# Attention and two feed-forward layers on one core: weights routed through PSUM, query sums copied by a DMA, one more key tile on GpSimd

## The chip, the cores and the metric

The kernel runs on one core of a Trainium2 chip. The metric is device time in microseconds (us) of one execution; lower is better. TensorE does the matmuls, VectorE (DVE), ScalarE (ACT) and GpSimd (POOL) the elementwise work, and SyncE (SP) issues all transfers. The granted TensorE clock was 0.999 of full speed over the profiled execution, which is its upper level, 2.4 GHz.

## The reference

```
q_pool = q.reshape(2, 8, 576, 2, 64).mean(axis=3)      # pairs of queries are averaged; seq is 1152
scores = q_pool @ k.transpose(0, 1, 3, 2) / sqrt(64)
attn = exp(scores - max); attn = attn / (sum(attn) + 1e-09)
x = (attn @ v), heads side by side                     # 1152 tokens x 512
h = x @ w_in (512 x 2048);   g = h if h >= 1, 0 if h <= -1, else (h+1)**2 / 4;   x = g @ w_out
h = x @ w_in2 (512 x 2048);  g = h * sigmoid(h);                                 out = g @ w_out2
```

Inputs are float32, except that the four weight matrices arrive in 64-bit form, two 32-bit words (`low`, `top`) a value.

## The kernel before

Every product is done with operands split into two parts (`hi` and `lo = x - hi`), and three or fewer of the four cross products, so each operand costs a copy and a subtraction. All work is first recorded as a list of `op(target, ways, deps, bufs, both)`: a way is an engine, how long the engine is held, the latency, and the function that emits the instructions. `plan_out` then lists them: again and again it takes the engine whose next piece could start first, by its own table of durations, free buffers (`room`) and due times, and writes the instructions in that order into each engine's queue. So a changed duration or rule reorders every engine; on the chip each queue runs in that order and waits where data are late.

- Attention runs over 16 heads. Of each head, `inputs` loads q, k and v and splits them: `split_q` adds the two queries of a pair (written twice side by side, `qs`, so that one transpose gives two stacked copies), PE transposes, and `qm` holds the query parts. `scores` multiplies 128 queries by 3 x 384 keys into a PSUM bank, DVE takes it out with a running minimum (L562), ACT does the exponential (L575).
- `values` takes the 9 key tiles of a head one by one: 4 PE transposes into a bank (L610), then `split` into the parts `thl`, then the matmuls with `vhl` (L618). `KINDS` says for each key tile how `split` goes. "psum": ACT writes `hi` from the bank (L588), DVE subtracts from the bank (L589). "pool": ACT copies the bank to `pf` (L593), GpSimd makes `hi` (L594) and `lo` (L135). Queries left over from two heads form `tails`, scaled in `ztail` (L670). `invert` adds 1e-9 to the sums on GpSimd (L687) and inverts them on DVE.
- Six PSUM banks (`b`) are shared by all of this; two more (`y`) hold the running output.
- The weights of a group of the hidden layer (there are 8, `w` = 0 to 7) come in quarters of 128 x 512. `weight_tasks` rebuilds float32 from the two words: ACT takes the absolute value (`size`, L102), DVE does `clamp` (L105), `shift` (L109), `sign` (L113) and `rest` (L117) on the tile `wf` in SBUF, ACT makes `hi` (L125), GpSimd `lo` (L135). The eight quarters of group 0 are worked off during attention, four of w_in between the heads and four of w_out at its end; those of groups 1 to 7 during the feed-forward part.
- The feed-forward part is 96 steps, `gemm1` (L155) and `gemm2` (L200 and L202), with five elementwise operations between them. Its first four `gemm1` stand among the last head's work.

`both` marks a DVE operation that works on SBUF alone. The planner held such an operation back while it thought GpSimd busy:

```
if o.both and e == "DVE" and pool_until[0] <= s < pool_until[1]:
    s = pool_until[1]
```

Of the kernel before, what the change touches and what calls it, by code (L numbers as in the profile page):

```python
# [18 lines left out]
def fused_kernel(  # L19
# [36 lines left out]
    KINDS = ("psum", "pool", "psum", "pool", "psum", "pool", "psum", "pool", "psum")  # L56
# [20 lines left out]
    def weight_tasks(idx, kind, pools, RAWS):  # L77
# [6 lines left out]
        def quarter(c):  # L84
            st = {}

            def load():
                if c == 0:
                    wt[layer, g, kind] = [
                        parts.tile([P, 4, 512], F32R, tag=f"w{x}{kind}", name=f"w{x}{kind}") for x in "hl"  # L90
                    ]
                if kind == "i":
                    sv = src[c * P : (c + 1) * P, g * FG * 2 : (g + 1) * FG * 2]
                else:
                    sv = src[g * FG + c * P : g * FG + (c + 1) * P, :]
                raw = raws.tile([P, 512, 2], U32, tag="wr", name="wr", bufs=RAWS)
                nc.sync.dma_start(out=raw.rearrange("p f w -> p (f w)"), in_=sv)
                st["low"], st["top"] = raw[:, :, 0], raw[:, :, 1]

            def size():  # L100
                st["w"] = raws.tile([P, 512], F32, tag="wf", name="wf", bufs=RAWS)
                nc.scalar.activation(st["w"], st["top"].bitcast(F32), AF.Abs)  # L102

            def clamp():
                nc.vector.tensor_scalar(st["w"], st["w"], LEAST, MOST, ALU.max, ALU.min)  # L105

            def shift():
                wi = st["w"].bitcast(U32)
                nc.vector.tensor_scalar(wi, wi, 3, 0x3FFFFFF8, ALU.logical_shift_left, ALU.bitwise_and)  # L109

            def sign():
                wi = st["w"].bitcast(U32)
                nc.vector.scalar_tensor_tensor(wi, st["top"], 0xC0000000, wi, ALU.bitwise_and, ALU.bitwise_or)  # L113

            def rest():
                wi = st["w"].bitcast(U32)
# [12 lines left out]

            return load, size, clamp, shift, sign, rest, parts_of, part_hi, part_lo  # L130
# [131 lines left out]
    def plan_out():  # L262
# [21 lines left out]
        while len(made) < len(ops):  # L284
            best = None
            for e in engines:
                found = []
                for o, k, t in ready[e].values():
# [12 lines left out]
                    if o.both and e == "DVE" and pool_until[0] <= s < pool_until[1]:  # L301
                        s = pool_until[1]
# [14 lines left out]
            if e == "POOL":  # L317
                pool_until = (s, s + lat)
            made.append(o)
# [19 lines left out]
    with ExitStack() as at, ExitStack() as keys, ExitStack() as prep:  # L339
# [27 lines left out]
        ztail = fixed.tile([P, P], F32, name="ztail")  # L367
        room.update(qraw=2, kraw=2, vraw=1, khl=2, qs=2, kk=3, qm=2, qt=2, qtraw=2, qts=1, p=2 * NM, pt=1, thl=THL, pf=PF, vhl=2)
# [6 lines left out]
        def prepare():  # L375
            nc.vector.tensor_copy(ident_r, ident)
            nc.vector.tensor_add(jtail, ident[:, 0:D], ident[:, D : 2 * D])
# [22 lines left out]
        def inputs(h):  # L400
# [33 lines left out]
            for part in [slice(3 * g, 3 * g + 3) for g in range(3)] if h == 0 else [slice(0, KC)] * 1:  # L434
# [5 lines left out]
                if first:  # L440
                    ways.insert(0, ("DVE", 0.1 + 0.6 * n, 0.18 + 0.6 * n, lo(nc.vector)))
                klo.append(op(t1 + 0.01, ways, [khi[-1]], [kr, kb], both=first))
# [25 lines left out]
            def split_q(e):  # L468
                t = qraws[qr.slot]
                e.tensor_add(qss[qb.slot], *(t[:, :, r].unsqueeze(2).to_broadcast([P, NM, 2, D]) for r in range(2)))  # L470

            t3 = base(h - 2) - 0.1 * PERIOD
            ways = [("POOL", 1.25, 1.31, lambda: split_q(nc.gpsimd))]
            if first:
                ways.insert(0, ("DVE", 0.6, 0.69, lambda: split_q(nc.vector)))
            sq = op(t3, ways, [lq], [qr, qb], both=first)
# [157 lines left out]
        def tails(h):  # L634
# [35 lines left out]
            o2 = op(t1 + 0.4, ("DVE", 0.2, 0.28, lambda: nc.vector.tensor_scalar_mul(ztail, ztail, sums[key])), [o1, o_inv[key]], [zb], both=True)  # L670
# [9 lines left out]
        def invert(h):  # L680
# [88 lines left out]

        STAGES = (("ACT", 0.57, 0.672), ("DVE", 0.332, 0.42), ("DVE", 0.335, 0.427), ("DVE", 0.6, 0.69), ("DVE", 0.6, 0.69))  # L770
        w_last = [None]

        def weights(w, kind, times, deps):


            def get(n, m):
                if (w, kind) not in wsets:
# [4 lines left out]
                    wsets[w, kind] = weight_tasks(w, kind, pools, 1 if (w, kind) == (0, "i") else RAWS)  # L782
# [4 lines left out]
            made = []  # L787
            for n, t in enumerate(times):
                bufs = [Buf("w" if (w, kind) == (0, "i") else "raw"), *whole]
                prev = op(t - 5, ("SP", 2.0, 4.4, lambda n=n: get(n, 0)()), [*deps, w_last[0]], bufs)  # L790
                w_last[0] = prev
                for m, (e, occ, lat) in enumerate(STAGES):
                    prev = op(t + 0.3 * m, (e, occ, lat, lambda n=n, m=m: get(n, m + 1)()), [prev], bufs, both=e == "DVE")
# [114 lines left out]
```

## Time and profile before

| | us |
|---|---|
| median of 3 runs | 695.96 (695.18 to 696.7) |
| profiled execution | 693.9 |
| its span, first to last instruction | 692.1 |
| TensorE busy in the span | 678.8 (98%) |
| VectorE, GpSimd, ScalarE busy | 547.1, 431.2, 413.7 |

A row of the trace names a source line, the engine, the operation and the tiles it writes and reads (`out<-in`). An engine's "idle before" is time in which it had nothing running; the name behind the arrow is what ended it. Matmuls are pipelined, so a busy TensorE is not one at its peak.

### The profile page before, as it was taken

To read this page: it belongs to the slowest core of one execution; us is meant where nothing else is said; L and a number is where in the kernel's file an instruction comes from. 1 tells how busy PE (TensorE), PEld (TensorE's weight loads), DVE (VectorE), ACT (ScalarE), POOL (GpSimd) and SP (SyncE) were. 2 spreads that over 40 slices of the span, in tenths; PEclk is the share of its full clock that TensorE was granted. 3 is DMA by queue.
4 is the path that set the end of the run, shared out by engine and by line. 5 is a ranking of instruction groups with operands and counts; after the bars stand their busy time and mean duration, and the time that the engine had idled before them with its cause. 6 is when DMAs were issued, how large, how long until landed. Compare 5 with 4: busy or idle time off the path is not lost.

```text
span 692.1 us, 11265 instructions
## 1 busy us (share of the span) xinstructions
PE 678.8 (98%) x3959; PEld 627.4 (91%) x3959; DVE 547.1 (79%) x1205; ACT 413.7 (60%) x773; POOL 431.2 (62%) x406
## 2 busy tenths in 40 slices
PE   8999999999999998999999999999999999999997
PEld 6898989888989997899999999999898999999896
DVE  7889989898888889658999796897884894993223
ACT  7988997968797887545544444454554543442221
POOL 7959897969796757735654455478664554453221
PEclk9999999999999999999999999999999999999999
DMA  7332231222110032102332232122131221200012
GB/s 210 109 92 59 92 112 38 79 72 65 50 49 11 26 124 76 62 31 92 122 123 91 92 106 79 61 92 92 62 121 62 92 93 60 93 30 1 1 45 92
DMA packets 28489, 52.93 MB, mean 76 GB/s; under 512 B 4752, under 2 KB 13968, under 8 KB 28432
## 3 DMA queue, kind: packets, MB, share of 16 engines
q1 hardware_dynamic: 28432, 52.21, 23.6%
q8 instruction: 31, 0.51, 0.3%
q14 instruction: 26, 0.21, 0.1%
HBM read 49.81 MB, written 2.39 MB: 75 GB/s over the span
## 4 chain that ended last, share of the span: by engine, by line
PE 81%; DVE 8%; POOL 7%; issue 2%; ACT 1%; DMA 0%; SPq 0%; POOLq 0%; DVEq 0%; ACTq 0%
PE bank L155 27%; PE bank L200 14%; PE bank L202 14%; PE bank L555 9%; PE bank L618 7%; PE bank L610 6%; DVE p L562 2%; POOL thl L135 2%; PE bank L656 2%; POOL xl L135 1%; POOL thl L594 1%; DVE thl L589 1%; PE bank L454 1%; PE bank L647 1%; DVE wf L113 1%
## 5 line engine op out<-in xcount | busy, mean ns | idle before, releaser
L135 POOL TENSOR_TENSOR gl<-gf,gh 128x384 fp32r<-128x384 f32 x96 | 112.4, 1171 | 119.2 <-ACT gh L184 117.5
L155 PE MATMUL bank<-xh,whi 128*128 128x384 f32 x384 | 129.2, 337 | 0.0
L155 PE MATMUL bank<-xl,whi 128*128 128x384 f32 x384 | 129.2, 336 | 0.0
L155 PE MATMUL bank<-xh,wli 128*128 128x384 f32 x384 | 128.9, 336 | 0.0
L562 DVE TENSOR_SCALAR_CACHE_REDUCE p<-bank 128x384 f32<-128x384 f32 x192 | 101.3, 550 | 18.8 <-PE bank L555 17.5
L618 PE MATMUL bank<-thl,vhl 128*128 128x512 f32 x288 | 112.4, 433 | 2.8 <-DVE thl L589 1.5
L178 DVE TENSOR_TENSOR gf<-bank,gf 128x384 f32<-128x384 f32 x96 | 52.9, 551 | 61.6 <-ACT gf L170 57.7
L555 PE MATMUL bank<-kk,qm 128*128 128x384 f32 x384 | 95.3, 352 | 1.9 <-DVE thl L589 1.7
L610 PE MATMUL bank<-ident,p 128*128 128x128 f32 x576 | 85.3, 273 | 0.0
L135 POOL TENSOR_TENSOR thl<-pf,thl 128x512 fp32r<-128x512 f32 x64 | 83.1, 1298 | 3.3
L575 ACT ACTIVATE p<-p,low 128x1152 f32<-128x1152 f32 x64 | 81.0, 1266 | 5.7 <-DVE low L572 5.5
L184 ACT CAST gh<-gf 128x384 fp32r<-128x384 f32 x96 | 49.4, 514 | 53.1 <-DVE gf L178 52.0
L113 DVE SCALAR_TENSOR_TENSOR wf<-wr,wf 128x512 uint32<-128x512 uint32 x64 | 76.2, 1191 | 1.2
L610 PEld LDWEIGHTS bank<-ident,p 128*128 128x128 f32 x576 | 69.4, 140 | 7.8 <-DVE thl L589 0.3
L555 PEld LDWEIGHTS bank<-kk,qm 128*128 128x128 f32 x384 | 65.4, 189 | 10.7 <-DVE thl L589 3.3
L155 PEld LDWEIGHTS bank<-xl,whi 128*128 128x128 f32 x384 | 72.1, 188 | 2.1
L155 PEld LDWEIGHTS bank<-xh,whi 128*128 128x128 f32 x384 | 72.1, 188 | 2.0
L155 PEld LDWEIGHTS bank<-xh,wli 128*128 128x128 f32 x384 | 72.1, 188 | 0.0
L589 DVE TENSOR_TENSOR thl<-bank,thl 128x512 fp32r<-128x512 f32 (+1 forms) x104 | 66.8, 653 | 3.6 <-ACT thl L588 3.3
L588 ACT CAST thl<-bank 128x512 fp32r<-128x512 f32 (+1 forms) x104 | 57.1, 562 | 20.6 <-PE bank L610 16.7
L170 ACT ACTIVATE gf<-bank 128x384 f32<-128x384 f32 x48 | 23.6, 492 | 76.5 <-PE bank L155 73.2
L135 POOL TENSOR_TENSOR wli<-wf,whi 128x512 fp32r<-128x512 f32 x32 | 43.1, 1347 | 41.7 <-ACT whi L125 41.5
(90 smaller groups left out, 1537.7 us busy)
## 6 DMA issues: line engine op xcount, KB each, us to landing
wr<-in_moe_w_in_dram SPq DMA_DIRECT2D x32, 512.0 KB, 3.7
wr<-in_moe_w_out_dram SPq DMA_DIRECT2D x32, 512.0 KB, 3.3
kraw<-in_k_dram SPq DMA_DIRECT2D x16, 288.0 KB, 2.9
vraw<-in_v_dram SPq DMA_DIRECT2D x16, 288.0 KB, 2.8
qraw<-in_q_dram SPq DMA_DIRECT2D x16, 256.0 KB, 3.0
out_dram<-part SPq DMA_DIRECT2D x9, 256.0 KB, 2.0
rb<-row SPq DMA_DIRECT2D x16, 128.0 KB, 3.3
qtraw<-in_q_dram SPq DMA_DIRECT2D x16, 32.0 KB, 2.5
```

What stands on the lines that cost most here:

```text
L113: nc.vector.scalar_tensor_tensor(wi, st["top"], 0xC0000000, wi, ALU.bitwise_and, ALU.bitwise_or)
L135: eng.tensor_sub(out, whole, hi.bitcast(F32))
L155: nc.tensor.matmul(ps, lhsT=w[:, c, j * P : (j + 1) * P], rhs=a[:, c, ts_], start=(c == 0 and n == 0), stop=(c == ND - 1 and n == 2),)
L200: nc.tensor.matmul(ps[:, :TB], lhsT=w[:, j, m * P : (m + 1) * P], rhs=a, start=start, stop=stop)
L202: nc.tensor.matmul(ps, lhsT=a[:, m * P : (m + 1) * P], rhs=w[:, j, :], start=start, stop=stop)
L555: nc.tensor.matmul(ps, lhsT=qq[:, c0 : c0 + P], rhs=rhs, start=n == 0, stop=n == last)
L562: nc.vector.tensor_scalar(dst, ps, -1.0, None, ALU.mult, ALU.min, accum_out=mxs[key, t][:, j : j + 1])
L575: nc.scalar.activation(pt(), pt(), AF.Exp, bias=lows[key][:, tt : tt + 1], scale=-1.0, accum_out=sums[key][:, tt : tt + 1])
L588: o1 = op(target, ("ACT", 0.477 * f, 0.587 * f, lambda: nc.scalar.copy(th(), ps())), deps, [bank, tb])
L589: o2 = op(target + 0.3, ("DVE", 0.6 * f, 0.683 * f, lambda: nc.vector.tensor_sub(tl(), ps(), th().bitcast(F32))), [o1], [bank, tb])
L610: nc.tensor.transpose(banks[bank.slot][:, i * P : (i + 1) * P], ps_[p_of[h, i].slot][:, c * P : (c + 1) * P], ident)
L618: nc.tensor.matmul(banks[6 + yb.slot], lhsT=lhsT, rhs=thls[tb.slot][i], start=not count, stop=len(count) == 2 * KC - 1)
```

## The change

- `clamp` and `shift` of group 0's quarters write a PSUM bank (`via`), `sign` works on it, `rest` reads it and writes `wf` again. The bank is one of the six (`b`), held from `clamp` to `rest`. All other groups stay in SBUF.
- The planner lets a `both` operation of DVE hold GpSimd as well, and keeps it off GpSimd 0.1 us earlier. `FAR`, the costs of the PSUM route, are not `both`.
- `split_q` writes the sum once; a DMA on SP's queue copies it beside itself (not for head 0).
- The last of the nine key tiles of a head goes the "pool" way.
- The scaling of `ztail` and the addition of 1e-9 go to ACT; the low part of head 1's keys is GpSimd's alone.

```diff
-    KINDS = ("psum", "pool", "psum", "pool", "psum", "pool", "psum", "pool", "psum")
+    KINDS = ("psum", "pool", "psum", "pool", "psum", "pool", "psum", "pool", "pool")
...
             def clamp():
-                nc.vector.tensor_scalar(st["w"], st["w"], LEAST, MOST, ALU.max, ALU.min)
+                st["x"] = via[c]() if c in via else st["w"]
+                nc.vector.tensor_scalar(st["x"], st["w"], LEAST, MOST, ALU.max, ALU.min)
             def shift():
-                nc.vector.tensor_scalar(wi, wi, 3, 0x3FFFFFF8, ALU.logical_shift_left, ALU.bitwise_and)
+                nc.vector.tensor_scalar(xi, xi, 3, 0x3FFFFFF8, ALU.logical_shift_left, ALU.bitwise_and)
             def sign():
-                nc.vector.scalar_tensor_tensor(wi, st["top"], 0xC0000000, wi, ALU.bitwise_and, ALU.bitwise_or)
+                nc.vector.scalar_tensor_tensor(xi, st["top"], 0xC0000000, xi, ALU.bitwise_and, ALU.bitwise_or)
             def rest():
-                nc.vector.scalar_tensor_tensor(wi, st["low"], 29, wi, ALU.logical_shift_right, ALU.bitwise_or)
+                nc.vector.scalar_tensor_tensor(wi, st["low"], 29, xi, ALU.logical_shift_right, ALU.bitwise_or)
...
-                    if o.both and e == "DVE" and pool_until[0] <= s < pool_until[1]:
+                    if o.both and e == "DVE" and pool_until[0] - 0.1 <= s < pool_until[1]:
...
             if e == "POOL":
                 pool_until = (s, s + lat)
+            elif o.both and e == "DVE":
+                free["POOL"] = max(free["POOL"], s + lat - 0.1)
...
+                if h:
+                    e.tensor_add(qss[qb.slot][:, :, 0], t[:, :, 0], t[:, :, 1])
...
+                twice = lambda: nc.sync.dma_start(out=qss[qb.slot][:, :, 1], in_=qss[qb.slot][:, :, 0])
...
-            o2 = op(t1 + 0.4, ("DVE", 0.2, 0.28, lambda: nc.vector.tensor_scalar_mul(ztail, ztail, sums[key])), [o1, o_inv[key]], [zb], both=True)
+            o2 = op(t1 + 0.4, ("ACT", 0.17, 0.28, lambda: nc.scalar.mul(ztail, ztail, sums[key])), [o1, o_inv[key]], [zb])
...
-                o = op(t0, ("POOL", 0.284, 0.23, lambda: nc.gpsimd.tensor_scalar_add(sums[key], sums[key], 1e-9)), deps)
+                o = op(t0, ("ACT", 0.1, 0.21, lambda: nc.scalar.activation(sums[key], sums[key], AF.Identity, bias=tiny)), deps)
...
+        FAR = (("ACT", 0.57, 0.672), *[("DVE", 0.6, 0.69)] * 4)
...
+                bank = Buf("b")
+                if not w:
+                    via[n] = lambda bank=bank: banks[bank.slot]
...
+                for m, (e, occ, lat) in enumerate(STAGES if w else FAR):
+                    more = bufs if w or not m else [*bufs, bank]
+                    prev = op(t + 0.3 * m, (e, occ, lat, lambda n=n, m=m: get(n, m + 1)()), [prev], more, both=e == "DVE" and w > 0)
```

The plan moves instructions everywhere in the attention part; from the second third of the first feed-forward layer on TensorE's order is the same. Three places matter below. The first is VectorE's queue at the fourth w_in quarter of group 0. Before, `rest` (L117) stood straight ahead of a key tile's subtraction (L589):

```order
L629 TENSOR_TENSOR y_143<-bank_77,pf_139 64x512
L572 TENSOR_REDUCE low<-mx 128x1
L117 SCALAR_TENSOR_TENSOR wf<-wr,wf 128x512
L589 TENSOR_TENSOR thl_133<-bank_73,thl_132 128x512
L677 TENSOR_TENSOR xl<-bank_71,xh 128x64
```

In the changed kernel the same quarter (`sign` is L115, `rest` L119, the subtraction L600) stands so in VectorE's queue, its intermediate in a bank:

```order
L600 TENSOR_TENSOR thl_137<-bank_75,thl_136 128x512
L115 SCALAR_TENSOR_TENSOR bank_74<-wr,bank_74 128x512
L573 TENSOR_SCALAR p_126,mx<-bank_70 128x384
L119 SCALAR_TENSOR_TENSOR wf<-wr,bank_74 128x512
L640 TENSOR_TENSOR y_142<-bank_77,pf_139 64x512
L600 TENSOR_TENSOR thl_131<-bank_73,thl_130 128x512
```

The operation still has a subtraction behind it; what moved is the tile that it reads and writes. `clamp` of this quarter stands 12 rows ahead of L115, and bank_74 is held from there to L119.

The second place is TensorE's queue at the last key tile of the last head, whose second part is thl_133. Before, its matmul (L618) came ahead of the first `gemm2` (L200):

```order
L618 MATMUL bank_77<-thl_132,vhl_141 128x512
L618 MATMUL bank_77<-thl_131,vhl_141 128x512
L618 MATMUL bank_77<-thl_133,vhl_141 128x512
L200 MATMUL bank_70<-gh,who 128x384
L200 MATMUL bank_70<-gl,who 128x384
```

In the changed kernel (L629 for L618, L202 for L200) nine matmuls of `gemm2` stand between the two parts of that tile:

```order
L629 MATMUL bank_77<-thl_132,vhl_141 128x512
L202 MATMUL bank_71<-gh,who 128x384
L202 MATMUL bank_71<-gl,who 128x384
L202 MATMUL bank_71<-gh,wlo 128x384
L202 MATMUL bank_72<-gh,who 128x384
L202 MATMUL bank_72<-gl,who 128x384
L202 MATMUL bank_72<-gh,wlo 128x384
L202 MATMUL bank_73<-gh,who 128x384
L202 MATMUL bank_73<-gl,who 128x384
L202 MATMUL bank_73<-gh,wlo 128x384
L629 MATMUL bank_77<-thl_133,vhl_141 128x512
```

The wait for thl_133 moved behind work that doesn't need it.

The third place is SP's queue around one head's copy of the query sums. Before:

```order
L97 DMA wr<-in_moe_w_in_dram 128x1024
L700 DMA row<-sum 128x4
L703 DMA rb_145<-row 64x512
L414 DMA qraw_98<-in_q_dram 128x4x128
L429 DMA vraw_105<-in_v_dram 128x576
```

And in the changed kernel (L711 and L714 are the sums' two transfers, L420 and L435 the loads of q and v):

```order
L711 DMA row<-sum 128x4
L97 DMA wr<-in_moe_w_in_dram 128x1024
L714 DMA rb_144<-row 64x512
L484 DMA qs_108<-qs_108 128x4x64
L420 DMA qraw_98<-in_q_dram 128x4x128
L435 DMA vraw_105<-in_v_dram 128x576
```

The copy (L484) waits on SP for GpSimd's addition, and the next loads of q and v stand behind it.

## Rows read from the trace of the kernel before

**Rows 1.** Windows, attention part: length, busy us of PE, PEld, DVE, ACT, POOL.

```profile
0.00:292.00 292.00, 283.78 (x1853) 253.03 (x1854) 253.99 (x780) 240.61 (x441) 233.26 (x245) 1.00 0.27 79
...
120.00:160.00 40.00, 36.95 (x241) 32.02 (x240) 35.54 (x105) 33.02 (x63) 33.62 (x33) 1.00 0.24 69
260.00:292.00 32.00, 28.86 (x175) 25.56 (x174) 27.16 (x57) 20.45 (x40) 24.86 (x24) 1.00 0.23 71
```

**Rows 2.** Timeline of TensorE, eight stretches: start, length, in brackets idle and releaser.

```profile
148.92 0.45 PE L454 MATMUL bank<-ident_r,khl 128*128 128x128 f32 x3 [0.70 <-DVE p L562]
...
159.22 0.62 PE L555 MATMUL bank<-kk,qm 128*128 128x384 f32 x2 [1.72 <-DVE thl L589]
...
261.28 0.44 PE L555 MATMUL bank<-kk,qt 128*128 128x384 f32 x1 [0.58 <-DVE low L572]
...
266.97 0.43 PE L675 MATMUL bank<-jtail,ztail 128*128 128x64 f32 x2 [0.60 <-DVE ztail L670]
...
273.41 0.50 PE L618 MATMUL bank<-thl,vhl 128*128 128x512 f32 x1 [0.76 <-DVE thl L589]
...
284.69 0.50 PE L618 MATMUL bank<-thl,vhl 128*128 128x512 f32 x1 [0.53 <-POOL thl L135]
...
290.04 0.49 PE L618 MATMUL bank<-thl,vhl 128*128 128x512 f32 x1 [0.64 <-DVE thl L589]
...
357.48 0.44 PE L200 MATMUL bank<-gh,who 128*128 128x384 f32 x1 [0.83 <-DVE part L214]
```

**Rows 3.** Timeline ahead of 159.22: VectorE, then GpSimd.

```profile
156.49 2.07 DVE L117 SCALAR_TENSOR_TENSOR wf<-wr,wf 128x512 uint32<-128x512 uint32 x1
...
156.47 1.54 POOL L720 TENSOR_TENSOR y<-y,rb 128x512 f32<-128x512 f32 x1 [0.18 <-DVE y L629]
157.97 1.74 POOL L470 TENSOR_TENSOR qs<-qraw 128x512 f32<-128x512 f32 x1
```

**Rows 4.** Groups of VectorE by line and form, 0 to 292 us.

```profile
L589 DVE TENSOR_TENSOR thl<-bank,thl 128x512 fp32r<-128x512 f32 x96 | 65.2, 684 | 3.6 <-ACT thl L588 3.3
...
L117 DVE SCALAR_TENSOR_TENSOR wf<-wr,wf 128x512 uint32<-128x512 uint32 x8 | 10.5, 1308 | 0.0
L113 DVE SCALAR_TENSOR_TENSOR wf<-wr,wf 128x512 uint32<-128x512 uint32 x8 | 9.2, 1151 | 0.0
L109 DVE TENSOR_SCALAR wf<-wf 128x512 uint32<-128x512 uint32 x8 | 5.9, 733 | 0.0
...
L105 DVE TENSOR_SCALAR wf<-wf 128x512 f32<-128x512 f32 x8 | 4.2, 532 | 0.0
```

**Rows 5.** Line 105 alone, same stretch: shortest, median and longest duration in ns.

```profile
L105 DVE TENSOR_SCALAR wf<-wf x8: 394/414/1174, 58.5 to 269.3; 128x512 f32<-128x512 f32 x8
```

**Rows 6.** Groups of GpSimd by line and form, 0 to 292 us.

```profile
L135 POOL TENSOR_TENSOR thl<-pf,thl 128x512 fp32r<-128x512 f32 x64 | 83.1, 1298 | 3.3
L594 POOL CAST thl<-pf 128x512 fp32r<-128x512 f32 x64 | 42.5, 663 | 24.3 <-ACT pf L593 21.6 <-PE bank L610 2.3
...
L470 POOL TENSOR_TENSOR qs<-qraw 128x512 f32<-128x512 f32 x15 | 19.7, 1320 | 4.4 <-PE bank L481 3.6 <-DMA qraw<-in_q_dram 0.7
...
L687 POOL TENSOR_SCALAR sum<-sum 128x4 f32<-128x4 f32 x16 | 3.9, 245 | 6.5 <-ACT p L575 5.7
...
L687 POOL TENSOR_SCALAR sum<-sum 128x1 f32<-128x1 f32 x8 | 2.3, 287 | 0.9 <-DVE wf L109 0.3
```

**Rows 7.** Waits of TensorE, 0 to 292 us: total, times, longest.

```profile
PE bank L618 <- POOL thl L135: 0.8, 2, 0.5
PE bank L454 <- DVE p L562: 0.7, 1, 0.7
...
PE bank L618 <- POOL thl L594: 0.4, 2, 0.2
```

**Rows 8.** Chain that ended last, in order of time: start, length, what.

```profile
293.05 4.22 PE bank L200 x24
```

**Rows 9.** DMA issues: KB each, median us to landing.

```profile
rb<-row SPq DMA_DIRECT2D x16, 128.0 KB, 3.3
```

More of the change, by code (lines that the diff above doesn't have):

```diff
@@ L75, in fused_kernel, with weight_tasks @@
     wt = {}
-    def weight_tasks(idx, kind, pools, RAWS):
+    def weight_tasks(idx, kind, pools, RAWS, via):
         layer, g = seq[idx]
@@ L367, in fused_kernel @@
         ztail = fixed.tile([P, P], F32, name="ztail")
+        tiny = fixed.tile([P, 1], F32, name="tiny")
         room.update(qraw=2, kraw=2, vraw=1, khl=2, qs=2, kk=3, qm=2, qt=2, qtraw=2, qts=1, p=2 * NM, pt=1, thl=THL, pf=PF, vhl=2)
@@ L376, in prepare @@
             nc.vector.tensor_copy(ident_r, ident)
+            nc.vector.memset(tiny, 1e-9)
             nc.vector.tensor_add(jtail, ident[:, 0:D], ident[:, D : 2 * D])
@@ L439, in inputs @@
                 ways = [("POOL", 0.2 + 1.175 * n, 0.25 + 1.18 * n, lo(nc.gpsimd))]
-                if first:
+                if not h:
                     ways.insert(0, ("DVE", 0.1 + 0.6 * n, 0.18 + 0.6 * n, lo(nc.vector)))
-                klo.append(op(t1 + 0.01, ways, [khi[-1]], [kr, kb], both=first))
+                klo.append(op(t1 + 0.01, ways, [khi[-1]], [kr, kb], both=not h))
             if h:
@@ L469, in split_q @@
                 t = qraws[qr.slot]
-                e.tensor_add(qss[qb.slot], *(t[:, :, r].unsqueeze(2).to_broadcast([P, NM, 2, D]) for r in range(2)))
+                if h:
+                    e.tensor_add(qss[qb.slot][:, :, 0], t[:, :, 0], t[:, :, 1])
+                else:
+                    e.tensor_add(qss[qb.slot], *(t[:, :, r].unsqueeze(2).to_broadcast([P, NM, 2, D]) for r in range(2)))
             t3 = base(h - 2) - 0.1 * PERIOD
[L473 to L476, printed above, removed]
+            if h:
+                sq = op(t3, ("POOL", 0.7, 0.76, lambda: split_q(nc.gpsimd)), [lq], [qr, qb])
+                twice = lambda: nc.sync.dma_start(out=qss[qb.slot][:, :, 1], in_=qss[qb.slot][:, :, 0])
+                sq = op(t3 + 1, ("SP", 0.5, 2.6, twice), [sq], [qb])
+            else:
+                sq = op(t3, [("DVE", 0.6, 0.69, lambda: split_q(nc.vector)), ("POOL", 1.25, 1.31, lambda: split_q(nc.gpsimd))], [lq], [qr, qb], both=True)
             t4 = base(h - 2) + 0.3 * PERIOD
@@ L786, in weights @@
             whole = [Buf("w" + kind)] if w else []
-            made = []
+            made, via = [], {}
             for n, t in enumerate(times):
                 bufs = [Buf("w" if (w, kind) == (0, "i") else "raw"), *whole]
+                bank = Buf("b")
+                if not w:
+                    via[n] = lambda bank=bank: banks[bank.slot]
                 prev = op(t - 5, ("SP", 2.0, 4.4, lambda n=n: get(n, 0)()), [*deps, w_last[0]], bufs)
                 w_last[0] = prev
-                for m, (e, occ, lat) in enumerate(STAGES):
-                    prev = op(t + 0.3 * m, (e, occ, lat, lambda n=n, m=m: get(n, m + 1)()), [prev], bufs, both=e == "DVE")
+                for m, (e, occ, lat) in enumerate(STAGES if w else FAR):
+                    more = bufs if w or not m else [*bufs, bank]
+                    prev = op(t + 0.3 * m, (e, occ, lat, lambda n=n, m=m: get(n, m + 1)()), [prev], more, both=e == "DVE" and w > 0)
                 prev = op(t + 2, ("ACT", 0.51, 0.61, lambda n=n: get(n, 7)()), [prev], bufs)
```

8 lines of the change are left out of this document (4 added, 4 removed).

## The prediction

> **What bounds the kernel now.** I read the windows first. TensorE is busy for 678.8 of the 692.1 us of the span. After 292 us, where the feed-forward part begins, it is short of work only at 357.48 (0.83 us) and once more by less. The attention part before that has 292 - 283.78 = 8.22 us of idle TensorE, and it lies in few places: 40 - 36.95 = 3.05 us in the window from 120 to 160, and 32 - 28.86 = 3.14 us in the window from 260 to 292 [rows 1]. The stretch between these two and the one from 20 to 120 are at TensorE's pace. So no change here can bring much more than some 8 us, unless it takes work from TensorE, which this one doesn't.
>
> Then I read TensorE's timeline for the places in question. Seven idle stretches in the two windows, of 0.53 to 1.72 us, are ended by VectorE six times and by GpSimd once [rows 2]. The timelines of these two engines say what came ahead. Before the longest one, at 159.22, VectorE spends 2.07 us on one `rest` (L117), from 156.49 on. GpSimd runs L720 and then L470 in that time, the latter in 1.74 us [rows 3]. The subtraction L589 for which TensorE waits stands straight behind `rest`, and TensorE starts when it is done. L117 has a mean of 1308 ns there, L113 one of 1151, while L589, of the same 128x512 and with one operand in PSUM, has 684 [rows 4]. L105 takes between 394 and 1174 ns for the same work [rows 5]; L470 has a mean of 1320 against its 1.74 [rows 6]. I read this as VectorE and GpSimd holding each other up when both work on SBUF alone, and a form that reads PSUM as free of it. The planner's table has 0.69 us for L117, so it let the transposed scores behind it come late.
>
> **The change, part by part.** All sums are made against the profiled execution, 693.9 us, whose span is 692.1; the median of the runs shown is 695.96, 2.06 more, and I add that at the end.
>
> *Weights through a bank.* A quarter's four operations now take 532 + 733 + 1151 + 1308 = 3724 ns [rows 4, 5]. Through PSUM I price each like L589: 4 x 684 = 2736 ns. That is 0.99 us a quarter, 7.9 us of VectorE for eight, none of it on TensorE's path by itself. What counts is the long operation ahead of a wait. Six of the stretches, 0.70 + 1.72 + 0.58 + 0.60 + 0.76 + 0.53 = 4.89 us [rows 2], stand where quarters are worked off; the seventh, at 290.04, comes below. The nearest row for the new forms is L589, which also writes SBUF; nothing in this trace writes a bank from VectorE with weights in it. Bounds: nothing comes back (0), or all idle of both windows, 3.05 + 3.14 = 6.19. I take -4.9.
>
> One rule speaks against this part. L105 undisturbed takes 394 to 414 ns [rows 5], and L589 684 [rows 4]. The Trainium skill, VectorE: DVE Perf Modes, section Why PSUM operands drop a tier, says that an fp32 operation with any operand in PSUM loses the mode that uses both SBUF ports, and does one element a cycle. By it, `clamp` and `shift` through a bank can't keep their short form: 16 x (0.684 - 0.414) = 4.3 us more of VectorE than if nothing disturbed them. The measured means, with the disturbance, leave a gain in the sum of four. If the disturbance had been absent where it mattered, this part would be worth 0.
>
> *One more key tile for GpSimd.* Sixteen tiles move from ACT and VectorE's L589 to ACT and GpSimd's L594 and L135. Each costs GpSimd 663 + 1298 = 1961 ns [rows 6], 31.4 us together, and frees 16 x 0.684 = 10.9 us of VectorE. A tile's parts are ready 1.961 - 0.684 = 1.28 us later. GpSimd is given back about half of L470, by elements written 0.66 us of 1.32, 15 x 0.66 = 9.9, and L687's 16 x 0.245 = 3.9 [rows 6] (eight smaller ones left out). So it goes from 233.26 to 233.3 + 31.4 - 9.9 - 3.9 = 250.9 us of 292, 86% [rows 1]. VectorE goes from 253.99 to 254.0 - 10.9 - 7.9 = 235.2, 81%. GpSimd becomes the fullest of the three helpers. The 64 tiles that go this way now cost TensorE 0.8 + 0.4 = 1.2 us of waits in all [rows 7], 0.02 each, since the planner puts other matmuls between. Sixteen more at that price are 0.3; with GpSimd's idle share nearly a third smaller (20% to 14%) I take +1.0. Bounds: 0, and all of the latency uncovered, 16 x 1.28 = 20.5.
>
> *The last tile of the last head.* It is where a longer latency would show, as there is little attention work behind it. At 290.04 TensorE waits 0.64 us for L589 [rows 2]. In the new order nine matmuls of `gemm2` stand between the two parts. Such a matmul takes 4.22 / 24 = 0.176 us [rows 8], so they cover 1.58 us, more than the 1.28. I take 0: one wait for another. Without that cover it would be +1.28.
>
> *The copy of the query sums.* A head's `qs` is complete later by the copy: half an addition (0.66) and a transfer of 128 KB that I price like the one of rb, of the same size, 3.3 us to landing [rows 9], against 1.32 before: 0.66 + 3.3 - 1.32 = +2.6 us. `qs` is not in the list of what TensorE waits for [rows 7], because the planner makes it a head ahead; 0. Behind it on SP's queue stand the next loads of q and v, and nothing late depends on them within a head. Uncovered it would be 15 x 2.6 = 39 us, a bound that I leave out of the range, since a whole head of other matmuls lies between.
>
> *The planner's rule.* In the feed-forward part weights stay in SBUF. There the rule can only move VectorE's operations away from GpSimd's. At 357.48 TensorE loses 0.83 us to VectorE [rows 2]; I give it half, -0.4. The move of `ztail` and the 1e-9 to ACT costs ACT under 10 us of the 292 - 240.61 that it has free [rows 1]: 0.
>
> Sum: -4.9 + 1.0 + 0 + 0 - 0.4 = -4.3. The profiled execution comes to 689.6, the median to 691.7.
>
> **The rivals.** *The disturbance stays* (or was not the cause). GpSimd is busier, and if `rest` still runs long because it writes SBUF and reads `wr` there, the stretches remain: -0.4 + 1.0, about 696. Against it: L589 also reads one SBUF operand and writes SBUF, and its mean of 684 stands among the same GpSimd work [rows 4]. The Trainium skill, SBUF — State Buffer, section Who interferes with whom, says that only a port pair shared by VectorE and GpSimd contends, as an exclusive lock; by that an operation that needs one SBUF read and one write of its own is free of it. The trace agrees for L589; no row shows it for an operation that writes a bank. Chance 0.10, between 694.6 and 697.
>
> *GpSimd becomes the bound* (the other side). At 86% mean it will be at its limit in stretches where heads overlap with weights, and TensorE then waits for L135 at many of the sixteen tiles. With x us exposed at each the result is -5.3 + 16x: slower by more than can be measured from x = 0.42 on (16 x 0.42 = 6.7). At 0.5 it is +2.7, 698.7. For it: two waits on L135 already [rows 7]. Against it: these are 0.8 in all, and the planner chooses matmuls by GpSimd's durations. 0.09.
>
> *A bank is missing.* For each quarter one of the six banks is held while 8 to 14 rows of VectorE's queue go by, at about 0.68 each some 8 us [rows 4], 64 us for eight. If TensorE were held by banks all that time it would lose a sixth, 10.7 us; half of that gives -4.3 + 5.4 = +1.1, 697.0. For it: a wait of 0.7 us on `p` L562, which empties a bank [rows 7]. Against it: it is the only long one that ends on taking scores out. 0.07, half of it slower.
>
> **How the numbers follow.** The forecast, faster, has a chance of 0.74 and a range of its own of 687.5 to 694.4: from all of 6.19 and 0.83 and a bit of start-up returned to less than half of the 4.9, where it would no longer be told from no change. A measurement of this kernel can tell about 0.2%, 1.4 us. Faster by more than that 0.74, within it 0.14 (the first rival and half of the third, 0.10 + 0.035), slower 0.12 (the second and the other half). The range reaches to 696.5, which takes in the first rival and leaves out the second; below it stops at 687.5, as there is no more idle time to give back.
>
> **What the profile after would show.** Right: windows with nearly no idle of TensorE around the two stretches of weights; the four operations at 0.6 to 0.75 us each with a longest near the mean; L135 on `thl` about 80 times and waits of TensorE on it below 2 us in all; GpSimd near 250 us and VectorE near 235 in the attention part. Wrong: `rest` with single values over 1 us; waits on `thl` of GpSimd at 0.3 us or more, many times; waits of TensorE on banks held by weights; a late transpose of `qs`; or a start-up that got longer, for which I have no row.

## The result, and the profile after

The changed kernel took 685.62 us (median of 4 runs, 685.51 to 685.7), the kernel before 695.73 in the same comparison (695.18 to 696.7): a ratio of 0.9853, interval 0.9836 to 0.987. That is 10.1 us faster, below the range of 687.5 to 696.5. The profiled execution went from 693.9 to 685.5, its span from 692.1 to 683.7.

The windows of the changed kernel (columns as in [rows 1]):

```profile
0.00:292.00 292.00, 288.42 (x1899) 260.76 (x1900) 236.89 (x757) 249.62 (x480) 242.91 (x254) 1.00 0.31 85
120.00:160.00 40.00, 39.85 (x267) 36.13 (x267) 32.78 (x112) 36.39 (x71) 37.87 (x38) 1.00 0.29 76
260.00:292.00 32.00, 31.95 (x198) 29.84 (x198) 17.52 (x39) 19.05 (x39) 22.37 (x23) 1.00 0.20 71
```

In the attention part TensorE has 292 - 288.42 = 3.58 us of idle time left, of 8.22 before. From 120 to 160 it is 0.15 of 3.05, from 260 to 292 0.05 of 3.14. But 4.64 us of idle time don't make a span shorter by 8.4. The busy times of the whole span, of the kernel before and of the changed one, say more:

```profile
PE 678.8 (98%) x3959; PEld 627.4 (91%) x3959; DVE 547.1 (79%) x1205; ACT 413.7 (60%) x773; POOL 431.2 (62%) x406
...
PE 675.4 (99%) x3959; PEld 627.2 (92%) x3959; DVE 519.4 (76%) x1180; ACT 421.3 (62%) x807; POOL 442.4 (65%) x414
```

TensorE was idle for 692.1 - 678.8 = 13.3 us before and for 683.7 - 675.4 = 8.3 after, 5.0 less. The other 3.4 us came out of its busy time, for the same 3959 matmuls. The count of matmuls says the same of the attention part: 1899 of them are done by 292 us, 46 more than the 1853 of [rows 1]. At 292 / 1899 = 0.154 us each that is an estimate of 7.1 us. It holds even where next to nothing was idle. From 20 to 120, before and after, 14 more matmuls are done, while the idle time fell only from 0.22 to 0.08 us:

```profile
20.00:120.00 100.00, 99.78 (x669) 89.88 (x668) 89.43 (x279) 87.13 (x160) 82.52 (x86) 1.00 0.28 81
...
20.00:120.00 100.00, 99.92 (x683) 91.28 (x681) 89.03 (x283) 91.43 (x177) 87.78 (x91) 1.00 0.37 96
```

TensorE's list of waits for the whole span has six entries, of which three are longer than 0.5 us:

```profile
PE bank L396 <- POOL thl L378: 1.5, 1, 1.5
PE bank L566 <- DVE qm L499: 0.6, 1, 0.6
PE bank L204 <- POOL gl L137: 0.6, 1, 0.6
PE bank L566 <- DVE xl L688: 0.4, 1, 0.4
PE bank L202 <- POOL gl L137: 0.4, 1, 0.4
PE bank L621 <- DVE thl L600: 0.4, 1, 0.4
```

None is a wait for GpSimd's `thl` during attention (L396, 1.5, is in the start-up), and `part` of 357.48 [rows 2] is gone. The four weight operations, with shortest, median and longest duration in ns, one list for each line:

```profile
L107 DVE TENSOR_SCALAR bank<-wf x8: 681/688/693, 59.4 to 262.5; 128x512 f32<-128x512 f32 x8
...
L111 DVE TENSOR_SCALAR bank<-bank x8: 694/696/700, 61.6 to 263.6; 128x512 uint32<-128x512 uint32 x8
...
L115 DVE SCALAR_TENSOR_TENSOR bank<-wr,bank x8: 673/689/694, 62.7 to 264.6; 128x512 uint32<-128x512 uint32 x8
...
L119 DVE SCALAR_TENSOR_TENSOR wf<-wr,bank x8: 680/684/689, 63.8 to 265.9; 128x512 uint32<-128x512 uint32 x8
```

No value is above 700, where L105 alone reached 1174 [rows 5] and L117 2070 [rows 3]. GpSimd's groups over the attention part:

```profile
L137 POOL TENSOR_TENSOR thl<-pf,thl 128x512 fp32r<-128x512 f32 x80 | 103.6, 1300 | 3.0
L605 POOL CAST thl<-pf 128x512 fp32r<-128x512 f32 x80 | 49.2, 620 | 23.2 <-ACT pf L604 19.8 <-PE bank L629 2.8 <-PE bank L667 0.2
...
L477 POOL TENSOR_TENSOR qs<-qraw 128x256 f32<-128x256 f32 x15 | 11.2, 748 | 4.6 <-PE bank L492 4.2 <-DMA qraw<-in_q_dram 0.2
```

The half sum takes 748 ns against 1320 [rows 6]. GpSimd is busy for 242.91 us in this part, VectorE for 236.89 (forecast 250.9 and 235.2).

Where did the time that the idle columns don't show hide? One place in the kernel before, in TensorE's timeline:

```profile
47.16 0.63 PE L618 MATMUL bank<-thl,vhl 128*128 128x512 f32 x2
...
52.87 0.47 PE L618 MATMUL bank<-thl,vhl 128*128 128x512 f32 x1
53.36 0.44 PE L555 MATMUL bank<-kk,qm 128*128 128x384 f32 x1
```

Two L618 in a row take 0.63 us together, the single one 0.47: they overlap, and the second begins some 0.2 after the first. At 52.87 the next matmul comes 0.49 after an L618, yet no idle time is shown in front of it, as the end of the single one reaches nearly there. About a quarter of a microsecond is lost and counted as busy. The Trainium skill, Perfetto Trace Analysis, section Identifying the Most-Contended Engine, calls TensorE's busy share a poor measure of how near it is to its limit, since its instructions are pipelined; this row agrees.

### The profile page after: what moved, and what is told of

It is laid out like the page before. It is cut to its first block, busy times and chain, and to the rows that moved or that the text cites. A ratio compares the mean times of both kernels' runs of the same rounds, so it can differ in the third digit from the quotient of the medians.

```text
span 683.7 us, 11372 instructions
## 1 busy us (share of the span) xinstructions
PE 675.4 (99%) x3959; PEld 627.2 (92%) x3959; DVE 519.4 (76%) x1180; ACT 421.3 (62%) x807; POOL 442.4 (65%) x414
## 4 chain that ended last, share of the span: by engine, by line
PE 87%; DVE 8%; POOL 2%; issue 2%; ACT 1%; DVEq 0%; POOLq 0%; ACTq 0%
PE bank L157 26%; PE bank L204 14%; PE bank L202 12%; PE bank L566 11%; PE bank L629 9%; PE bank L621 8%; PE bank L667 3%; DVE p L573 1%; PE bank L460 1%; PE bank L658 1%; PE bank L492 1%; DVE wf L119 1%; DVE wf L107 1%; DVE part L216 1%; POOL xl L137 1%
## 5 line engine op out<-in xcount | busy, mean ns | idle before, releaser
L629 PE MATMUL bank<-thl,vhl 128*128 128x512 f32 x288 | 113.6, 435 | 0.0
L137 POOL TENSOR_TENSOR thl<-pf,thl 128x512 fp32r<-128x512 f32 x80 | 103.6, 1300 | 3.0
L621 PE MATMUL bank<-ident,p 128*128 128x128 f32 x576 | 85.0, 273 | 0.4 <-DVE thl L600 0.4
L621 PEld LDWEIGHTS bank<-ident,p 128*128 128x128 f32 x576 | 69.1, 140 | 8.7 <-DVE thl L600 0.8
L137 POOL TENSOR_TENSOR wlo<-wf,who 128x512 fp32r<-128x512 f32 x32 | 46.0, 1437 | 35.4 <-ACT who L127 35.4
L137 POOL TENSOR_TENSOR wli<-wf,whi 128x512 fp32r<-128x512 f32 x32 | 44.6, 1394 | 34.0 <-ACT whi L127 32.6
L202 PE MATMUL bank<-gl,who 128*128 128x384 f32 x192 | 64.9, 338 | 0.4 <-POOL gl L137 0.4
L202 PE MATMUL bank<-gh,who 128*128 128x384 f32 x192 | 65.1, 339 | 0.0
```

Of the source, the lines that this page charges most:

```text
L137: eng.tensor_sub(out, whole, hi.bitcast(F32))
L202: nc.tensor.matmul(ps[:, :TB], lhsT=w[:, j, m * P : (m + 1) * P], rhs=a, start=start, stop=stop)
L621: nc.tensor.transpose(banks[bank.slot][:, i * P : (i + 1) * P], ps_[p_of[h, i].slot][:, c * P : (c + 1) * P], ident)
L629: nc.tensor.matmul(banks[6 + yb.slot], lhsT=lhsT, rhs=thls[tb.slot][i], start=not count, stop=len(count) == 2 * KC - 1)
```

## The experiments

Medians in us; the ratio is to the kernel before in the same comparison (its interval in brackets), whose own median lay between 694.3 and 695.5. Between kernels of different comparisons less than about 1 us is not relied on.

| kernel | us | ratio (interval) |
|---|---|---|
| changed, order kept, weights in SBUF (e1) | 695.92 | 1.001 (0.9998 to 1.0021) |
| changed, without the route through PSUM (e2) | 702.7 | 1.0117 (1.0101 to 1.0133) |
| before + route (e3) | 690.12 | 0.9933 (0.9918 to 0.9947) |
| before + rule (e4) | 688.23 | 0.9913 (0.9897 to 0.9929) |
| changed, without the rule (e5) | 685.38 | 0.9864 (0.985 to 0.9879) |
| before + key tile (e6) | 695.01 | 1.0005 (0.9995 to 1.0014) |
| changed, without the key tile (e7) | 686.51 | 0.9881 (0.9866 to 0.9896) |
| changed, without the copy (e9) | 686.05 | 0.9874 (0.9858 to 0.989) |
| changed, without both small moves (e10) | 688.95 | 0.99 (0.9886 to 0.9915) |
| before + route + small moves (e11) | 692.38 | 0.9957 (0.994 to 0.9973) |
| before + route + key tile (e12) | 691.92 | 0.9942 (0.9928 to 0.9957) |
| changed, w_out quarters later (e13) | 689.1 | 0.9896 (0.988 to 0.9913) |
| changed, clamp in SBUF (e14) | 687.63 | 0.9882 (0.9867 to 0.9896) |
| changed, ztail on VectorE (e15) | 686.91 | 0.9877 (0.9862 to 0.9892) |
| changed, 1e-9 on GpSimd (e16) | 689.82 | 0.992 (0.9905 to 0.9935) |

**The route through PSUM.** The theory is that of the prediction: VectorE and GpSimd hold each other up where both work on SBUF alone. The rival: the new order and the moved work bring the gain, and the place of the intermediate costs nothing.

```diff
-                st["x"] = via[c]() if c in via else st["w"]
+                st["x"] = st["w"]
```

> The changed kernel with every instruction in the same place of every queue, but clamp, shift, sign and rest of group 0 work on the SBUF tile again instead of the bank (the bank stays reserved). If the gain came from taking VectorE's weight operations out of GpSimd's way, the disturbance is back: L115 and L119 at 1.1 to 1.3 us mean with single values over 1.5, GpSimd's rows beside them stretched, and 689.5 to 692, of 685.6 for the changed kernel. If the gain came from the new order and from the work moved between engines, it stays at 685 to 687, as the tile's place then costs nothing.

It took 695.92, the whole gain back, with every instruction in its place. VectorE's groups of this kernel:

```profile
L600 DVE TENSOR_TENSOR thl<-bank,thl 128x512 fp32r<-128x512 f32 x80 | 54.4, 687 | 7.5 <-ACT thl L599 6.2 <-POOL qts L522 0.2
...
L119 DVE SCALAR_TENSOR_TENSOR wf<-wr,wf 128x512 uint32<-128x512 uint32 x8 | 9.3, 1164 | 0.0
L111 DVE TENSOR_SCALAR wf<-wf 128x512 uint32<-128x512 uint32 x8 | 8.2, 1030 | 0.0
L115 DVE SCALAR_TENSOR_TENSOR wf<-wr,wf 128x512 uint32<-128x512 uint32 x8 | 7.8, 971 | 0.0
L107 DVE TENSOR_SCALAR wf<-wf 128x512 f32<-128x512 f32 x8 | 6.4, 804 | 0.0
```

The four take 1164 + 1030 + 971 + 804 = 3969 ns a quarter, against 4 x 0.69 in the changed kernel: 1.2 us more, 9.7 us for eight quarters. The execution that these rows come from took 694.36, 8.9 more than the changed kernel's 685.51; the medians differ by 10.3. L600, which reads a bank, is at 687 as ever. GpSimd is held up too, though less: its cast L605 has a mean of 661 ns here, of 620 in the changed kernel. The rival is out, and the size was expected at about half of this.

Without the route in the planner too (bank and `FAR` taken out, all weights `both`):

```diff
-                for m, (e, occ, lat) in enumerate(STAGES if w else FAR):
-                    more = bufs if w or not m else [*bufs, bank]
+                for m, (e, occ, lat) in enumerate(STAGES):
+                    more = bufs
```

> The changed kernel without the route through PSUM, the planner knowing it: group 0 in SBUF with the short durations of its table and kept off GpSimd by the new rule. If the route is what pays, 688.5 to 692, with single weight operations still over 1 us. If the planner's rule alone keeps the two engines apart, or the order and the moved work pay, 685 to 687.

702.7 is above both expectations. TensorE waits 7.2 us in two places, 3.6 each. The timeline of one of them, of VectorE, GpSimd and TensorE:

```profile
138.91 6.13 DVE L107 TENSOR_SCALAR wf<-wf 128x512 f32<-128x512 f32 x1
144.97 0.54 DVE L573 TENSOR_SCALAR_CACHE_REDUCE p<-bank 128x384 f32<-128x384 f32 x1
...
137.01 2.55 POOL L137 TENSOR_TENSOR thl<-pf,thl 128x512 fp32r<-128x512 f32 x2
139.50 0.62 POOL L605 CAST thl<-pf 128x512 fp32r<-128x512 f32 x1
140.08 1.42 POOL L137 TENSOR_TENSOR khl<-kraw,khl 128x576 fp32r<-128x576 f32 x1
141.46 1.27 POOL L137 TENSOR_TENSOR thl<-pf,thl 128x512 fp32r<-128x512 f32 x1
142.69 0.72 POOL L477 TENSOR_TENSOR qs<-qraw 128x256 f32<-128x256 f32 x1
143.37 1.39 POOL L137 TENSOR_TENSOR vhl<-vraw,vhl 128x576 fp32r<-128x576 f32 x1
...
145.58 0.62 PE L460 MATMUL bank<-ident_r,khl 128*128 128x128 f32 x3 [3.57 <-DVE p L573]
```

One `clamp` of 128x512 holds VectorE for 6.13 us. It ends 0.28 us after GpSimd's row of instructions, whose last ends at 143.37 + 1.39 = 144.76: five of them without a gap and the rest of a sixth, which was under way. These keep their usual durations. The Trainium skill, SBUF — State Buffer, section Who interferes with whom, has the shared port pair held by whoever issues first for the whole instruction, the other blocked. By that `clamp` would wait for the one under way, of 2.55 / 2 = 1.28 us at most; the trace shows a wait for five more. The measurement decides: a VectorE operation of this kind can wait for a whole row. TensorE stands 3.57 us until VectorE's next result.

The two waits are not all of the loss. Behind each of them the granted clock of TensorE, the number behind the five engines in these windows, is at its lower level for a while (0.50 of full speed, 1.2 GHz):

```profile
145.00:151.00 6.00, 5.42 (x22) 4.88 (x23) 4.95 (x14) 2.79 (x5) 1.89 (x2) 0.50 0.37 101
152.00:158.00 6.00, 6.00 (x45) 5.45 (x44) 5.98 (x16) 3.95 (x8) 4.21 (x5) 1.00 0.04 12
```

TensorE does 22 matmuls in the first six us and 45 in the second. Of the 700.3 - 683.7 = 16.6 us by which the span is longer than the changed kernel's, 9.3 are idle time of TensorE and 7.3 busy time (682.7 against 675.4).

The same route put into the kernel before, alone (the diff's lines on `via`, `bank` and `FAR`, of which this is the core):

```diff
+                st["x"] = via[c]() if c in via else st["w"]
+                nc.vector.tensor_scalar(st["x"], st["w"], LEAST, MOST, ALU.max, ALU.min)
```

> The kernel before with only the route through PSUM for group 0. If taking these operations out of GpSimd's way is most of the gain, 688 to 691 and the idle stretches of TensorE in 120 to 160 and 260 to 292 nearly gone. If it is the order, the moved work or the rule, 694 to 697.

690.12, 4.8 less than before by the medians and 3.8 by the profiled executions (693.9 and 690.12), within what was expected of the theory. Its windows:

```profile
120.00:160.00 40.00, 39.60 (x261) 35.10 (x260) 36.34 (x117) 36.54 (x70) 36.79 (x37) 1.00 0.30 82
260.00:292.00 32.00, 30.99 (x191) 27.84 (x191) 22.51 (x55) 19.47 (x39) 18.88 (x21) 1.00 0.21 71
```

Idle from 120 to 160 falls from 3.05 to 0.40, from 260 to 292 only to 1.01.

One operation alone taken back to SBUF in the changed kernel, in its order:

```diff
-                nc.vector.tensor_scalar(st["x"], st["w"], LEAST, MOST, ALU.max, ALU.min)
+                nc.vector.tensor_scalar(st["w"], st["w"], LEAST, MOST, ALU.max, ALU.min)
...
-                nc.vector.tensor_scalar(xi, xi, 3, 0x3FFFFFF8, ALU.logical_shift_left, ALU.bitwise_and)
+                nc.vector.tensor_scalar(xi, wi, 3, 0x3FFFFFF8, ALU.logical_shift_left, ALU.bitwise_and)
```

> The changed kernel in its order, only clamp of group 0 writes the SBUF tile again (shift reads it and writes the bank, sign and rest as changed). clamp alone took 0.39 us undisturbed in the kernel before, less than the 0.69 through the bank. If a VectorE operation on SBUF alone has to wait for the end of GpSimd's run of instructions, L107 has single values of 1.2 us and more and the kernel takes 687 to 689; if only operations with two SBUF inputs are held up, L107 is at 0.4 throughout and the kernel takes 684.5 to 685.6.

687.63, 2.0 slower. L107 of this kernel, in the same columns as above:

```profile
L107 DVE TENSOR_SCALAR wf<-wf x8: 415/696/1343, 59.4 to 264.4; 128x512 f32<-128x512 f32 x8
```

Undisturbed it is 0.27 faster than through the bank, at its worst 0.65 slower, and its median is no better. So an operation with one SBUF input is held up too, and the short form wins nothing here. This is what became of the rule that spoke against the route.

**The rule.** Alone in the kernel before:

```diff
-                    if o.both and e == "DVE" and pool_until[0] <= s < pool_until[1]:
+                    if o.both and e == "DVE" and pool_until[0] - 0.1 <= s < pool_until[1]:
...
+            elif o.both and e == "DVE":
+                free["POOL"] = max(free["POOL"], s + lat - 0.1)
```

> The kernel before with only the planner's rule (a VectorE operation on SBUF alone holds GpSimd as well, and keeps off it 0.1 us earlier). If the disturbance is the cause and can be planned around, 690 to 694, with L113 and L117 nearer 0.7 us. If a disturbance can't be planned around, since the chip's times differ from the table by more than 0.1 us, 694.5 to 697.

688.23: 6.7 less, more than the route alone, and less time than either expectation gave. Its groups, from an execution of 689.75:

```profile
L113 DVE SCALAR_TENSOR_TENSOR wf<-wr,wf 128x512 uint32<-128x512 uint32 x8 | 8.4, 1046 | 0.0
L117 DVE SCALAR_TENSOR_TENSOR wf<-wr,wf 128x512 uint32<-128x512 uint32 x8 | 7.2, 903 | 0.1
L105 DVE TENSOR_SCALAR wf<-wf 128x512 f32<-128x512 f32 x8 | 6.6, 840 | 0.0
L109 DVE TENSOR_SCALAR wf<-wf 128x512 uint32<-128x512 uint32 x8 | 6.0, 757 | 0.0
```

They sum to 3.55 us a quarter of 3.72, so the disturbance is mostly still there. The gain can't be the shorter operations alone; that the planner now reckons with the blocked engine and puts other work in the gaps is my reading, and no run shows it by itself. Taken out of the changed kernel (the same lines back):

> The changed kernel without the planner's new rule. With group 0 through PSUM, few operations of VectorE on SBUF alone are left during attention, so the rule should matter only where group 1 begins: if that is so, 685.5 to 687. If the rule is worth as much here as alone (the kernel before with only the rule took 688.2, 6.7 less), 690 or more.

685.38, no difference that these runs can tell. With the route in place the rule adds nothing. It can't replace the route there either, as e2 has the rule and takes 702.7. The kernel before with both, and nothing else, was not run.

**The key tile.** Put into the kernel before, and (the same line back) taken out of the changed one:

```diff
-    KINDS = ("psum", "pool", "psum", "pool", "psum", "pool", "psum", "pool", "psum")
+    KINDS = ("psum", "pool", "psum", "pool", "psum", "pool", "psum", "pool", "pool")
```

> The kernel before with only the last key tile of each head given to GpSimd. If a VectorE operation on SBUF waits until GpSimd's run of back-to-back instructions ends, a fuller GpSimd makes the waits longer: 696.5 to 702, with single weight operations of 2 us and more. If the tile only relieves VectorE, 692 to 695.

> The changed kernel with the last key tile on VectorE as before. The prediction priced the move to GpSimd at +1.0: then 684 to 685.2 here. If the move pays once nothing on VectorE waits for GpSimd (16 x 0.69 = 11 us of VectorE freed), 686.5 to 689.

In the kernel before it brings nothing (695.01, between the two expectations). Its two longest weight groups are like those of [rows 4]:

```profile
L113 DVE SCALAR_TENSOR_TENSOR wf<-wr,wf 128x512 uint32<-128x512 uint32 x8 | 10.6, 1326 | 0.1
...
L117 DVE SCALAR_TENSOR_TENSOR wf<-wr,wf 128x512 uint32<-128x512 uint32 x8 | 9.8, 1224 | 0.0
```

In the changed kernel it is worth 0.9 (686.51; by the ratios 0.9881 - 0.9853 of 695.7, 1.9), not a cost of 1.0. With the route alone:

> The kernel before with the route through PSUM and the last key tile on GpSimd, nothing else. In the kernel before the tile alone was worth nothing (695.0 of 694.3). If it pays once VectorE no longer waits for GpSimd, because VectorE is then full where weights are worked off (from 253 to 264 us it has no gap with the route alone): 686.5 to 688.5, of 690.1 with the route alone. If the tile is worth as little here, 689.5 to 691.

691.92 is 1.8 above the route alone by the medians, but only 0.6 by the ratios (0.9942 and 0.9933): no gain, and neither expectation. TensorE's weight loads (PEld, which overlap the matmuls) wait more for GpSimd:

```profile
PEld bank L619 <- POOL thl L595: 3.9, 13, 0.6
```

With the other part (L136) that is 4.6 us, against 1.9 with the route alone. So the tile pays, if at all, only with the rest.

**The copy.** Taken out of the changed kernel:

```diff
-                if h:
-                    e.tensor_add(qss[qb.slot][:, :, 0], t[:, :, 0], t[:, :, 1])
...
-                twice = lambda: nc.sync.dma_start(out=qss[qb.slot][:, :, 1], in_=qss[qb.slot][:, :, 0])
```

> The changed kernel with the query sums written twice by GpSimd again, no copy. The prediction priced the copy at 0 and the GpSimd time that it gives back only as a part of GpSimd's sum: 685 to 686.5. If GpSimd, fuller by 15 x (1.32 - 0.75) = 8.6 us, becomes late, 687 to 690, with more TensorE waits on GpSimd's thl.

686.05, 0.4 more (1.5 by the ratios). At most a small help, and no harm: qs lands 3.1 us after its issue, nearly as priced.

**The small moves.** Both undone, then one at a time, then both added to the kernel before with the route:

```diff
-            o2 = op(t1 + 0.4, ("ACT", 0.17, 0.28, lambda: nc.scalar.mul(ztail, ztail, sums[key])), [o1, o_inv[key]], [zb])
+            o2 = op(t1 + 0.4, ("DVE", 0.2, 0.28, lambda: nc.vector.tensor_scalar_mul(ztail, ztail, sums[key])), [o1, o_inv[key]], [zb], both=True)
...
-                o = op(t0, ("ACT", 0.1, 0.21, lambda: nc.scalar.activation(sums[key], sums[key], AF.Identity, bias=tiny)), deps)
+                o = op(t0, ("POOL", 0.284, 0.23, lambda: nc.gpsimd.tensor_scalar_add(sums[key], sums[key], 1e-9)), deps)
```

> The changed kernel with the scaling of ztail on VectorE again and the 1e-9 on GpSimd again. The prediction priced both moves at 0: 685 to 686.3. The kernel before with only the route through PSUM took 690.1, 4.5 more than the changed kernel, and taking away the tile (0.9), the copy (0.4) or the rule (none) one at a time doesn't fill that: if these small moves are the rest, 687.5 to 689 here.

> The changed kernel with the scaling of ztail alone on VectorE again (8 operations). With both small moves undone the kernel took 689.0, 3.3 more. If ztail is the cause (an operation of VectorE on SBUF alone, in front of TensorE's L686): 687.5 to 689. If GpSimd's 24 additions are: 685.3 to 686.5.

> The changed kernel with the addition of 1e-9 alone on GpSimd again (24 small operations, some 5.4 us of GpSimd). If they push back GpSimd's part of the key tiles, which TensorE met 10 times in the trace with both moves undone and not once in the changed kernel: 687.5 to 689. If ztail is the cause: 685.3 to 686.5.

> The kernel before with the route through PSUM (690.1) and both small moves to ScalarE. If the small moves are worth their 3.3 us by themselves: 686.5 to 687.8. If they are worth it only where the last key tile is GpSimd's too (with the route and the tile, 691.9): 689 to 690.5, no more than 1 us below the route alone.

Undone together they cost 3.3, ztail alone 1.3 (between its two expectations), the 1e-9 alone 4.2 (above both). So it is mainly the 24 additions on GpSimd, of 0.23 us each, priced at 0 because their place was taken to be free. The planner's order changes with them, and no run separates the two. With both undone, TensorE's list of waits has nothing on GpSimd during attention after the start-up, but that of its weight loads has. From 15 to 292 us, with both undone and then in the changed kernel:

```profile
PEld bank L629 <- POOL thl L605: 1.7, 7, 0.3
PEld bank L629 <- POOL thl L137: 1.3, 6, 0.3
...
PEld bank L629 <- POOL thl L605: 0.5, 2, 0.3
PEld bank L629 <- POOL thl L137: 0.2, 1, 0.2
```

So 3.0 us in 13 waits stand against 0.7 in 3 (the expectation of e16 has 10 and none). All of the loss shows as busy time of TensorE, 679.4 against 675.4. With the 1e-9 alone on GpSimd the weight loads also wait 2.4 us for ScalarE's copy `pf`, so not all of its 4.2 us goes through GpSimd's parts.

Added to the route alone they make the kernel slower, 692.38 of 690.12, against both expectations. Here are GpSimd, ScalarE and VectorE at one of two places, and TensorE's longest wait:

```profile
52.11 1.28 POOL L473 TENSOR_TENSOR qs<-qraw 128x512 f32<-128x512 f32 x1 [4.01 <-PE bank L484]
53.33 1.50 POOL L597 CAST thl<-pf 128x512 fp32r<-128x512 f32 x1
...
51.81 0.59 ACT L596 COPY pf<-bank 128x512 f32<-128x512 f32 x1
...
53.02 1.33 DVE L723 TENSOR_TENSOR y<-y,rb 128x512 f32<-128x512 f32 x1
...
PE bank L621 <- POOL thl L597: 2.2, 2, 1.1
```

`pf` is ready at about 52.4, but the cast L597 stands behind the query sum L473, which itself came late, after 4.01 us of waiting for TensorE to be done with the old `qs`. The cast takes 1.50 us itself, of 0.66 [rows 6], beside L723, which is VectorE's and works on SBUF alone. The new order gives VectorE four of these additions, where the route alone has one. I read this as the same disturbance, from another operation. In TensorE's list of waits L621 loses 2.2 us to it in two places. In the changed kernel this sum is the half one, of 0.75.

**A try at a faster one.** The w_out quarters of group 0 get later due times:

```diff
-        made[0, "o"] = weights(0, "o", [base(14) + 3 * n for n in range(4)], prepared + made[0, "i"][0])
+        made[0, "o"] = weights(0, "o", [base(14) + 4 + 5 * n for n in range(4)], prepared + made[0, "i"][0])
```

> The changed kernel with the due times of the four w_out quarters of group 0 set 4 us later and 5 instead of 3 us apart. If what TensorE still loses around 250 us (some 1.7 us) is VectorE's fullness there, 684 to 685.2; if the quarters then come late for the first gemm2, or the stretch only moves, 685.4 to 687.

689.1, above both expectations. The loss moved to where group 1 begins, a wait that the changed kernel doesn't have:

```profile
PE bank L202 <- DVE part L216: 2.6, 1, 2.6
```

Behind it the granted clock is 0.54 from 352 to 355 us, and TensorE does 10 matmuls there, against 19 from 356 to 359. Three of the four runs, at a granted clock of 0.997, took 689.1 to 689.2; the fourth, at 0.999, took 687.8.

The move of the low part of head 1's keys was not run by itself. No kernel that was run is clearly faster than the changed one.

## Why the prediction was wrong

- *What bounds the kernel.* The place was right, and the cause: the two stretches of weights are where the idle time went, and e1 and e2 show the two engines holding each other up. **The step that failed is taking TensorE's idle time for all that can be won:** "no change here can bring much more than some 8 us", and the whole sum in terms of idle stretches. The profiled execution was to come down by 4.3 us and came down by 8.4. The idle time itself came out nearly as summed: 4.9 + 0.4 = 5.3 us forecast, 5.0 measured. The other 3.4 us had been counted as busy: a late matmul starts under the pipelined end of the one before, also from 20 to 120, which the prediction had "at TensorE's pace". With the 1.0 that the key tile didn't cost, this is the miss of 4.1 in the profiled execution; the rest, 1.95, is in the step from profile to median below. The low end of the range doesn't follow from the idle time either: 695.96 - 8.22 - 0.83 is 686.9, not 687.5.
- *Weights through a bank.* Priced at 4 x 684 = 2736 ns, measured 688 + 696 + 689 + 684 = 2757 (medians). Alone it brought 4.8 of the 4.9 forecast; as the profiled executions differ by 3.8, the nearness is in part luck. But in the changed kernel the same route is worth 10.3 (e1; 8.9 in the profiled execution). The size of this term depends on the others, and I had added it to them as a constant. GpSimd is fuller there (247.56 us of 292 in e1, 85%, against 80% before); that this is the reason is my reading, as the order differs too.
- *The key tile.* +1.0 forecast; it measured 0.9 to 1.9 the other way in the changed kernel. Of the 1.28 us of latency little showed: no wait of TensorE on GpSimd's `thl` is left in attention, and its weight loads wait 0.7 us for it in all. Rival two, GpSimd as the bound, fails with it; its mechanism shows in e12, where these loads wait 4.6.
- *The small moves.* Priced at 0, worth 3.3: next to the route the largest mis-sized term. ScalarE did have the room, but I looked only at what the move costs there, not at what it gives back on GpSimd, where each addition stands ahead of a key tile's part.
- *The copy, the last tile, the rule at 357.48.* Right in sign: 0.4 for the copy; the wait of 290.04 is gone; the 0.83 of 357.48 is gone whole, not by half (without the rule, in e5, TensorE waits 0.3 on `part` again).
- *From profile to median.* I added 2.06, and this alone puts the time outside the range: without it the low end, 687.5, stands for a profiled execution of 685.44, and that took 685.51. The changed kernel's profiled execution is at its median, 685.51 and 685.62, so 1.95 of the 6.1 us missed is in this step. The kernel before ran from 693.6 to 697.2 in one comparison of 17 runs, e1 from 694.2 to 696.6, while the changed kernel's four lie within 0.2 us and e3's six within 0.44. Part of that spread goes with the granted clock. Of the 44 runs of the kernel before beside the experiments, the 36 at 0.999 or more have a median of 694.7, the 8 below that one of 696.2; in e1 five at 0.999 or more took 694.2 to 695.0, seven at 0.996 to 0.998 took 695.8 to 696.6. The changed kernel's four are all at 1.0. In e2 and e13 the clock fell behind a long wait of TensorE; no kept trace shows that in the kernel before, so why it is lower in some of its runs is not shown.
- *Other rivals.* That the disturbance stays is excluded by the four medians; that a bank is missing by TensorE's list of waits, which names none held by weights (with the route alone, e3, it has one on `rest`, of 0.7 us).

The single terms, each taken out of the changed kernel, sum to more than the gain, and added to the route alone two of them have the other sign. What each is worth by itself stays open to the planner's order, which every edit changes.

## What to carry to other kernels

Count the matmuls done by a time, or the distance of their starts, before taking TensorE's idle time as the most that can be won. Where VectorE and GpSimd share work, look for single VectorE values far above the shortest of their form: a route through PSUM made each of these operations 0.69 us with hardly a spread, and was worth 4.8 us in one kernel and 10.3 in another with a fuller GpSimd. Look at the granted clock behind a long wait of TensorE, as the wait may not be all that it cost. When a move is priced, ask for both ends: what it costs the engine that takes it, and what stood behind it on the engine that gives it away.

## What the runs showed of the hardware

An operation of VectorE on SBUF alone that takes 0.4 us undisturbed took 6.13 us while GpSimd ran instructions back to back, and GpSimd wasn't slowed in that row (e2). Elsewhere GpSimd was: a cast that has a median of 0.61 us took 1.50 beside a VectorE addition on SBUF alone (e11). With one operand or the result in PSUM, and one SBUF operand at most, no such operation took more than 0.70 us in the changed kernel.

After TensorE had waited 3.57 us (e2) its granted clock was 0.50, 1.2 GHz, from 145 to 151 us, with half as many matmuls done as in the next six us at 1.00. After a wait of 2.59 us (e13) it was 0.54 from 352 to 355. After the 1.72 us of [rows 2] it stayed at 1.00.
